# Top-k attention and an ELU feed-forward block on one core: nine transposes issued in one run, and both rows' distances formed by one GpSimd operation

## The chip, the core and the metric

The kernel runs on one core of a Trainium2 chip. The core has five engines that run their own instruction queues in order and meet through semaphores: TensorE (PE; its weight loads are shown apart as PEld), VectorE (DVE), ScalarE (ACT), GpSimd (POOL) and SyncE (SP, which issues DMAs here). The metric is the device time of one execution in microseconds; lower is better.

## The reference, cut to what matters

```python
def _attn_ref(q, k, v):                       # (8, 8, 576, 64) each
    scores = (1 / np.sqrt(64)) * np.matmul(q, k.transpose(0, 1, 3, 2))
    kth = np.partition(scores, -32, axis=-1)[..., -32:-31]
    scores = np.where(scores >= kth, scores, -1000000000.0)
    scores = scores - np.max(scores, axis=-1, keepdims=True)
    attn = np.exp(scores)
    attn = attn / (np.sum(attn, axis=-1, keepdims=True) + 1e-09)
    return np.matmul(attn, v)

def _moe_ref(x, w_in, w_out):                 # (4608, 512), (512, 2048), (2048, 512)
    h = x @ w_in
    g = np.where(h > 0.0, h, np.exp(np.minimum(h, 0.0)) - 1.0)
    return g @ w_out
```

The attention output, with its heads side by side, is `x` of the second function. All values are fp32 on the chip; the two weight matrices arrive as 64-bit floats and are decoded in the kernel.

## The kernel before

**Tiling.** For each of 8 batches the queries are cut into four tiles of 128 and one remainder of 64. A *step* is one tile and one pair of heads: `i = 0` and `i = 1` are the pair's two heads, called *row 0* and *row 1* here, each 128 x 576 scores that lie side by side in `u.sc`. A remainder's step holds four heads in two halves of the partitions. There are 144 steps. Two steps with the same pair of heads and neighbouring tiles form a *group*, whose attention product is computed at once (256 columns); remainders, and the first batch's tiles, form groups of their own.

**What a step goes through.** `scores` (L322) multiplies keys and queries into two PSUM tiles, `wide[0]` and `wide[1]`, and ACT copies them out (L339). `select` (L366) finds the 32nd largest score of each row on DVE: four rounds of MAX8 and between them three of MATCH_REPLACE8, for both rows. The first round's largest value is in `u.first`, the 32nd in `u.last`. `mask` (L389) works on one row: GpSimd forms `gap`, the 32nd score less the largest (L406); ACT then makes a steep ramp below the 32nd score (Prelu, L407) and the exponential, with its sum over the row in `u.den` (L408). `normalise` (L413) has GpSimd divide: five operations on 128 x 2 values (L418 to L423), one of them a power of 722 ns, and then one scaling of each row (L425). `turn` (L430) transposes 128 x 128 chunks of the two rows on PE (L444) and ACT copies each call's result from PSUM to the group's `et` (L445). The 1152 columns of two rows make nine chunks: `main` is chunks 0 to 3 (row 0), `rest` is chunk 4 (the last 64 columns of row 0 and the first 64 of row 1), `other` is chunks 5 to 8 (row 1). `main` and `other` take a tile of `ps_t`, a PSUM pool of two buffers that `attend` uses too; `rest` writes to spare columns of `wide[1]`. `attend` (L455) multiplies `et` with the values (L470), in pairs of row 0 and row 1, and `finish` copies the result to `xT` (L497).

**The feed-forward part.** When a block of 128 to 384 tokens has all its heads, its FFN pieces are put on a list. `hidden` multiplies with `w_in` (L545), and ACT makes the two halves of the ELU from PSUM (L555, L558) and an exponential (L560, mostly followed by a subtraction of one, L564). A *gate* closes the ELU with one addition: on GpSimd (L515) for most of the program, on DVE (L517) at the start and for the last block. `project` multiplies with `w_out` (L573), ACT copies the result (L582) and SP stores it. `feed`, called four times a step, closes the gates that are due and takes as many pieces from the list as the planner's shares allow. The pieces and their places come from fixed costs in the program, not from run time.

**What sets the order.** The first 8 steps (`tight`) have another loop, whose order is the framework's. From step 8 on, the order on PE, ACT, DVE and GpSimd is that of the source: in one round of the loop at L702 the selection of step `n` runs on DVE, the masks and the normalisation of step `n-1` on ACT and GpSimd, and the transposes of step `n-2` on PE. One round, as the queues see it:

- head: scores of step `n+2`, attention of a closed group
- feed 1, mask of row 0 of `n-1`, key and query transposes if any are due
- feed 2, `turn(done, main)`, `turn(done, rest)`, mask of row 1 of `n-1`
- feed 3, `turn(done, other)`
- normalisation of `n-1`, feed 4

Each engine takes its part of this list in order. A copy of `other` on ACT therefore stands behind the second mask's ramp and exponential and behind what feed 3 gave to ACT; a distance on GpSimd stands behind the gates that earlier feeds gave to GpSimd. For the early steps `mask` is called with `early=True`, where ACT forms the distance.

Of the kernel before, what the change touches and what calls it, by code (L numbers as in the profile page):

```python
# [9 lines left out]
ALU = mybir.AluOpType  # L10
FP32 = mybir.dt.float32
# [13 lines left out]
class Tile:  # L25
# [6 lines left out]
    def __init__(self, b, qt, rows, block, cols):  # L32
        self.b, self.qt, self.rem = b, qt, qt == 4
        self.rows = rows
        self.block = block
        self.cols = cols
        self.ql = cols.stop - cols.start
# [21 lines left out]
class Step:  # L59
# [7 lines left out]
    def __init__(self, t, hp, group, at):  # L67
        self.t, self.hp = t, hp
        self.group, self.at = group, at
        self.masked = self.normal = self.turned = False  # L70
        if t.rem:
            rows = [(4 * hp, 0), (4 * hp + 2, 0), (4 * hp + 3, 1), (4 * hp + 1, 1)]
            self.heads = [
                (h, i, slice(64 * (n % 2), 64 * (n % 2) + 64))
                for n, (h, i) in enumerate(rows)
            ]
        else:
            self.heads = [(2 * hp + i, i, slice(0, 128)) for i in range(2)]
# [3 lines left out]
def kernel(  # L82
# [9 lines left out]
    nc = tc.nc  # L92
    P = nc.NUM_PARTITIONS
    B, H, S, D = q.shape
    dm, dff = moe_w_in.shape[0], moe_w_in.shape[1] // 2
    J = S // P
# [15 lines left out]
    def pool(name, bufs, **kw):  # L112
        return ctx.enter_context(tc.tile_pool(name=name, bufs=bufs, **kw))
# [6 lines left out]
    small = pool("small", 4)  # L120
# [8 lines left out]
    early = raws.enter_context(tc.tile_pool(name="early", bufs=1))  # L129
# [69 lines left out]
    def hook():  # L199

        if not decode:
            return
        decode.pop(0)()
        if not decode:
            raws.close()
            late["f"] = ctx.enter_context(tc.tile_pool(name="f", bufs=2))
            late["g"] = ctx.enter_context(tc.tile_pool(name="g", bufs=2))
            late["x"] = ctx.enter_context(tc.tile_pool(name="xt", bufs=2))
            late["in"] = ctx.enter_context(tc.tile_pool(name="in", bufs=2))
# [103 lines left out]
    def turn_qk(whole=False):  # L313
        while turning:
            if next(turning[0], turning) is turning:
                turning.pop(0)
            elif not whole:
                return
# [3 lines left out]
    def scores(u):  # L322

        u.sc = scpool.tile([P, 2, S], FP32, tag="sc", name="sc")
        q0 = (QUERIES if u.t.b == 0 else S) + u.t.qt * P
        for half in range(2):
            for h, i, rows in u.heads:
                kq = kqT[u.t.b, h // 2]
                part = slice(i * D, (i + 1) * D)
                k0 = (KEYS if i == 0 and u.t.b == 0 else 0) + half * HS  # L330
                nc.tensor.matmul(  # L331
                    wide[i][rows, half, 0:HS],
                    kq[part, q0 : q0 + u.t.ql],
                    kq[part, k0 : k0 + HS],
                    start=True,
                    stop=True,
                )
        for i in range(2):
            nc.scalar.activation(  # L339
                u.sc[:, i, :].rearrange("p (a s) -> p a s", a=2),  # L340
                wide[i][:, :, 0:HS], AF.Copy, scale=scale,
            )
# [23 lines left out]
    def select(u):  # L366

        u.first = small.tile([P, 2, 8], FP32, tag="m1", name="m1")
        u.last = small.tile([P, 2, 8], FP32, tag="m4", name="m4")
        cur = [u.sc[:, i, :] for i in range(2)]  # L370
        found = [u.first[:, i, :] for i in range(2)]
        for i in range(2):
            nc.vector.max(found[i], cur[i])  # L373
        yield
        wk = [wkpool.tile([P, S], FP32, tag=f"wk{i}", name="wk")[:] for i in range(2)]
        for r in range(TOP_K // 8 - 1):
            for i in range(2):
                nc.vector.match_replace(wk[i], found[i], cur[i], TAKEN)  # L378
            cur = wk
            for i in range(2):  # L380
                if r < TOP_K // 8 - 2:
                    found[i] = small.tile([P, 8], FP32, tag=f"m{i}", name="m")[:]
                else:
                    found[i] = u.last[:, i, :]
                nc.vector.max(found[i], cur[i])  # L385
            hook()
            yield

    def mask(u, i, early=False):  # L389

        if u.masked:
            return
        if i == 0:
            u.den = small.tile([P, 4], FP32, tag="den", name="den")
        u.masked = i == 1  # L400
        sc, low, top = u.sc[:, i, :], u.last[:, i, 7:8], u.first[:, i, 0:1]
        gap = u.den[:, 2 + i : 3 + i]
        if early:
            nc.scalar.activation(gap, top, AF.Prelu, scale=-1.0, bias=low, alpha=1.0)
        else:
            nc.gpsimd.tensor_tensor(gap, low, top, ALU.subtract)  # L406
        nc.scalar.activation(sc, sc, AF.Prelu, scale=-1.0, bias=low, alpha=1.0 / STEEP)  # L407
        nc.scalar.activation(  # L408
            sc, sc, AF.Exp, scale=-STEEP, bias=gap, accum_out=u.den[:, i : i + 1]
        )  # L410

    def normalise(u):
# [16 lines left out]
    def turn(u, chunks):  # L429

        if u.turned:
            return
        g = u.group
        if g.et is None:
            g.et = etpool.tile([P, 2 * J + 1, len(g.tiles), P], FP32, tag="et", name="et")
        if chunks.stop - chunks.start == 1:
            ps = wide[1][:, 1, HS : HS + P]
        else:
            ps = ps_t.tile([P, JP], FP32, tag="t", name="eps")
        sc = u.sc[:, :, :].rearrange("p i s -> p (i s)")  # L440
        n = chunks.stop - chunks.start
        for c in range(n):
            c0 = (chunks.start + c) * P
            nc.tensor.transpose(ps[:, c * P : (c + 1) * P], sc[:, c0 : c0 + P], ident[:])  # L444
        nc.scalar.copy(  # L445
            g.et[:, chunks, u.at, :],
            ps[:, 0 : n * P].rearrange("p (c q) -> p c q", c=n),
        )
        if chunks.stop == 2 * J + 1:
            u.turned = True  # L450
            if u.at == len(g.tiles) - 1:
                closing.append(g)
# [149 lines left out]
    for b in range(B):  # L602
# [28 lines left out]
        for qts in order:  # L631
# [3 lines left out]
            for qt in qts:  # L635
                n = len(steps)
# [60 lines left out]
    def step(n):  # L697
        return steps[n] if 0 <= n < NS else None

    closing = []  # L700
    main, rest, other = slice(0, J), slice(J, J + 1), slice(J + 1, 2 * J + 1)
    for n in range(NS + 3):  # L702
        for fn, args in todo.pop(n, []):
            fn(*args)
        ahead, cur, prev, done = step(n + 2), step(n), step(n - 1), step(n - 2)
        if n < tight:
            turn_qk(True)
            if n < 3:
                scores(ahead)
            if n > 1:  # L710
                scores(step(n + 3))
            for i in range(2):
                passes = select_row(cur, i, n < tight - 1)
                next(passes)
                if i == 0:
                    while closing:
                        attend(closing.pop(0))
                elif prev:
                    normalise(prev)
                    turn(prev, main)  # L720
                    turn(prev, rest)
                    turn(prev, other)
                feed(n, 0.25)
                next(passes)
                mask(cur, i, True)
                feed(n, 0.25)
            continue
        if n == tight:
            ctx.enter_context(tc.manual_schedule(engines=engines))
        passes = select(cur) if cur else iter(range(4))  # L730
        if ahead and n > tight:
            scores(ahead)
        while closing:
            attend(closing.pop(0))
        next(passes)
        feed(n, 0.25)
        if prev:
            mask(prev, 0)
        turn_qk()
        next(passes)  # L740
        feed(n, 0.25)
        if done:
            turn(done, main)
            turn(done, rest)
        if prev:
            mask(prev, 1)
        next(passes)
        feed(n, 0.25)
        if done:
            turn(done, other)  # L750
        next(passes)
        if prev:
            normalise(prev)
        feed(n, 0.25)
        turn_qk(True)
# [36 lines left out]
```

## Time and profile before

| what | value |
|---|---|
| median of 3 runs | 1643.64 us (1641.84 to 1643.79) |
| the profiled execution | 1642.57 us |
| its span, first to last instruction | 1640.8 us |
| granted TensorE clock, mean | 0.974 |
| MAX8 on DVE (L385) | 816 of 752 ns |
| MATCH_REPLACE8 on DVE (L378) | 544 of 748 ns on the work copy, 272 of 748 ns on the scores |
| first FFN product on PE (L545) | 2432 of 374 ns |
| second FFN product on PE (L573) | 1152 of 599 ns |
| transposes on PE (L444) | 1152 of 279 ns into `ps_t`, 144 of 282 ns into `wide[1]` |
| copies of transposes on ACT (L445) | 288 of 571 ns, 144 of 269 ns |
| masks on ACT (L407, L408) | 288 of 782 ns, 288 of 776 ns |
| distances on GpSimd (L406) | 272 of 190 ns |
| scalings on GpSimd (L425) | 288 of 750 ns |
| gates on GpSimd (L515) | 119 of 1386 ns |

A profile shows one execution. Times in the timeline are counted from the span's start; a row there is a start, a length, the engine, the line of the source, the operation, output and inputs, how many equal instructions were merged, and in brackets how long the engine sat idle before it and what ended the idle time. The ends of matmuls are modelled, so that one that starts before its predecessor's end is the rule and not an error. PE lists 2432 first FFN products where the source has 1216, and twice the attention and second FFN products too, since each of these fp32 products is run as two instructions; a transpose is one. "A <- B" in a list of waits means that A waited and B ended it. The first 150 us are taken up by loading and decoding the weights, and there the granted clock is often half.

### The profile page before, as it was taken

What the parts mean: (1) busy time and instruction counts of PE and PEld (TensorE: products, weight loads), DVE (VectorE), ACT (ScalarE), POOL (GpSimd) and SP (SyncE); (2) the same over time, 40 slices, a digit from 0 to 9 for tenths busy, and PEclk for the clock granted to TensorE, in tenths of its full rate; (3) what the DMA queues carried; (4) which work ended last, traced back from release to release, by engine and by line L of the source; (5) the groups of instructions that cost most, each with busy time, mean ns of one, the idle gap of its engine ahead of it and who ended that gap; (6) DMA issues with size and microseconds to landing.
All of it is one profiled execution on the core that took longest, in us unless ns stands there. A gap on an engine that the chain in (4) does not pass through costs nothing.

```text
span 1640.8 us, 25344 instructions
## 1 busy us (share of the span) xinstructions
PE 1581.7 (96%) x8276; PEld 1011.8 (62%) x8276; DVE 1453.4 (89%) x2981; ACT 1187.7 (72%) x2400; POOL 708.7 (43%) x1534
## 2 busy tenths in 40 slices
PE   4788999999999999999999999999999999999999
PEld 3566777666575757555566666655557575755564
DVE  6987999999999999999999699999999599998000
ACT  6887778778695867778678686868759595958521
POOL 4775445445353534445335353535435353534300
PEclk8579999999999999999999999999999999999999
DMA  7431221012100310012100211012100201000000
GB/s 226 151 128 25 50 40 26 7 22 45 42 1 7 59 42 8 7 22 44 36 14 15 43 30 28 1 28 44 36 14 0 43 1 35 1 13 2 7 13 14
DMA packets 188037, 56.18 MB, mean 34 GB/s; under 512 B 178177, under 2 KB 179201, under 8 KB 187905
## 3 DMA queue, kind: packets, MB, share of 16 engines
q1 hardware_dynamic: 186704, 54.26, 14.1%
q8 instruction: 66, 1.08, 0.3%
q14 instruction: 67, 0.54, 0.1%
q10 hardware_dynamic: 1200, 0.30, 0.1%
HBM read 45.09 MB, written 9.44 MB: 33 GB/s over the span
## 4 chain that ended last, share of the span: by engine, by line
PE 76%; ACT 12%; DVE 7%; POOL 3%; issue 1%; DMA 1%; SPq 0%; ACTq 0%; DVEq 0%; POOLq 0%
PE ops L573 29%; PE hps L545 23%; PE avps L470 10%; PE scps L331 7%; PE eps L444 6%; DVE wk L378 3%; DVE m L385 3%; ACT sc L408 2%; ACT et L445 2%; ACT sc L407 2%; DVE m L373 1%; ACT n L564 1%; ACT n L555 1%; ACT sc L339 1%; ACT n L560 1%
## 5 line engine op out<-in xcount | busy, mean ns | idle before, releaser
L385 DVE MAX8 m<-wk 128x8 f32<-128x576 f32 x816 | 577.9, 752 | 0.3 <-POOL den L406 0.3
L545 PE MATMUL hps<-xT,w_in 128*128 128x256 f32 (+2 forms) x2432 | 545.8, 374 | 0.0
L573 PE MATMUL ops<-w_out,gT 128*128 128x512 f32 x1152 | 523.6, 599 | 0.0
L545 PEld LDWEIGHTS hps<-xT,w_in 128*128 128x128 f32 x2432 | 406.0, 192 | 100.1 <-issue 26.3
L378 DVE MATCH_REPLACE8 wk<-m,wk 128x576 f32<-128x576 f32 x544 | 401.4, 748 | 0.0
L573 PEld LDWEIGHTS ops<-w_out,gT 128*128 128x128 f32 x1152 | 209.0, 190 | 233.9 <-issue 232.8
L418 POOL TENSOR_SCALAR dene<-den 128x2 f32<-128x2 f32 x144 | 32.9, 228 | 686.5 <-ACT sc L408 686.1
L408 ACT ACTIVATE sc<-sc,den 128x576 f32<-128x576 f32 x288 | 223.6, 776 | 65.5 <-POOL den L406 44.2
L407 ACT ACTIVATE sc<-sc,m 128x576 f32<-128x576 f32 x288 | 225.3, 782 | 10.8 <-DVE m L385 10.7
L470 PE MATMUL avps<-et,vT 128*64 128x256 f32 (+2 forms) x2080 | 207.2, 330 | 17.4 <-ACT et L445 17.2
L425 POOL TENSOR_SCALAR sc<-sc,rec 128x576 f32<-128x576 f32 x288 | 213.0, 750 | 15.0 <-POOL rec L423 0.2
L331 PE MATMUL scps<-kqT 64*128 64x288 f32 (+1 forms) x1280 | 206.0, 442 | 13.6 <-ACT kqT L307 9.1
L339 ACT ACTIVATE sc<-scps 128x576 f32<-128x576 f32 x288 | 171.8, 647 | 65.1 <-PE scps L331 65.1
L445 ACT COPY et<-eps 128x512 f32<-128x512 f32 x288 | 164.6, 571 | 73.4 <-PE eps L444 73.4
L378 DVE MATCH_REPLACE8 wk<-m,sc 128x576 f32<-128x576 f32 x272 | 200.6, 748 | 0.0
L373 DVE MAX8 m<-sc 128x8 f32<-128x576 f32 x272 | 191.6, 749 | 8.8 <-ACT sc L339 8.8
L444 PEld LDWEIGHTS eps<-ident,sc 128*128 128x128 f32 x1152 | 144.9, 144 | 87.2 <-issue 52.7
L444 PE MATMUL eps<-ident,sc 128*128 128x128 f32 x1152 | 177.1, 279 | 13.7 <-POOL sc L425 13.7
L470 PEld LDWEIGHTS avps<-et,vT 128*64 128x64 f32 x2080 | 128.5, 142 | 98.8 <-ACT et L445 31.7
L515 POOL TENSOR_TENSOR gT<-n,gT 128x512 f32<-128x512 f32 (+1 forms) x119 | 164.9, 1386 | 31.2 <-ACT n L564 31.1
L331 PEld LDWEIGHTS scps<-kqT 64*128 64x128 f32 (+1 forms) x1280 | 111.3, 182 | 89.5 <-issue 43.8
L555 ACT ACTIVATE n<-hps 128x512 f32<-128x512 f32 (+1 forms) x156 | 87.3, 559 | 56.8 <-PE hps L545 56.0
(53 smaller groups left out, 1089.6 us busy)
## 6 DMA issues: line engine op xcount, KB each, us to landing
raw<-in_moe_w_in_dram SPq DMA_DIRECT2D x16, 512.0 KB, 6.1
vT<-in_v_dram SPq DMA_DIRECT2D x64, 128.0 KB, 2.5
raw<-in_moe_w_out_dram SPq DMA_DIRECT2D x16, 512.0 KB, 3.6
out_dram<-osb SPq DMA_DIRECT2D x32, 256.0 KB, 2.1
kin<-in_k_dram SPq DMA_DIRECT2D x112, 72.0 KB, 2.5
qin<-in_q_dram SPq DMA_DIRECT2D x112, 72.0 KB, 2.6
kin<-in_k_dram SPq DMA_DIRECT2D x8, 128.0 KB, 4.5
vT<-in_v_dram SPq DMA_DIRECT2D x64, 16.0 KB, 2.2
```

Of the source, the lines that this page charges most:

```text
L331: nc.tensor.matmul(wide[i][rows, half, 0:HS], kq[part, q0 : q0 + u.t.ql], kq[part, k0 : k0 + HS], start=True, stop=True,)
L373: nc.vector.max(found[i], cur[i])
L378: nc.vector.match_replace(wk[i], found[i], cur[i], TAKEN)
L385: nc.vector.max(found[i], cur[i])
L407: nc.scalar.activation(sc, sc, AF.Prelu, scale=-1.0, bias=low, alpha=1.0 / STEEP)
L408: nc.scalar.activation(sc, sc, AF.Exp, scale=-STEEP, bias=gap, accum_out=u.den[:, i : i + 1])
L425: nc.gpsimd.tensor_scalar(u.sc[:, i, :], u.sc[:, i, :], rec[:, i : i + 1], 1.0, ALU.mult, ALU.mult)
L444: nc.tensor.transpose(ps[:, c * P : (c + 1) * P], sc[:, c0 : c0 + P], ident[:])
L445: nc.scalar.copy(g.et[:, chunks, u.at, :], ps[:, 0 : n * P].rearrange("p (c q) -> p c q", c=n),)
L470: nc.tensor.matmul(ps[i * D : (i + 1) * D, cols], vt[:, 2 * J + i if c == J else i * J + c, :], w, start=(c == 0), stop=(c == J),)
L545: nc.tensor.matmul(blk.h[:, f % bank, :], w_in[:, i, f * P : (f + 1) * P], blk.xT[:, i, 0:n_tok], start=(i == 0), stop=(i == NC - 1),)
L573: nc.tensor.matmul(blk.o[:], blk.gT[f // NG][:, f % NG, s * P : (s + 1) * P], w_out[:, f, :], start=(f == 0), stop=(f == NF - 1),)
```

## The change

Two things are moved.

First, `turn(done, other)` is called right after `turn(done, main)` and ahead of `turn(done, rest)`, so that a step's nine transposes are issued in one run and their three copies stand on ACT ahead of the mask of row 1; it was called after feed 3. Since `other` is no longer the last of the three calls, `turn` counts the chunks that are left instead of asking for the last chunk's number.

Second, from step 9 on the distances of both rows are formed by one GpSimd operation on 128 x 2 values (a stride of 8 in `u.last` and `u.first`), at the head of the next round, ahead of feed 1 and its gates. It was one operation for each row, issued with that row's mask. The early steps keep the distances on ACT.

```diff
@@ Step.__init__
+        self.left = 9
@@ mask(u, i, early=False)
-        if i == 0:
+        if i == 0 and early:
             u.den = small.tile([P, 4], FP32, tag="den", name="den")
         u.masked = i == 1
         sc, low, top = u.sc[:, i, :], u.last[:, i, 7:8], u.first[:, i, 0:1]
         gap = u.den[:, 2 + i : 3 + i]
         if early:
             nc.scalar.activation(gap, top, AF.Prelu, scale=-1.0, bias=low, alpha=1.0)
-        else:
-            nc.gpsimd.tensor_tensor(gap, low, top, ALU.subtract)
...
+    def distance(u):
+
+        if u.masked:
+            return
+        u.den = small.tile([P, 4], FP32, tag="den", name="den")
+        nc.gpsimd.tensor_tensor(
+            u.den[:, 2:4], u.last[:, :, 7], u.first[:, :, 0], ALU.subtract
+        )
@@ turn(u, chunks)
-        if chunks.stop == 2 * J + 1:
+        u.left -= n
+        if u.left == 0:
             u.turned = True
@@ the loop over n, from step 8 on
+        if prev:
+            distance(prev)
         passes = select(cur) if cur else iter(range(4))
...
         if done:
             turn(done, main)
+            turn(done, other)
             turn(done, rest)
         if prev:
             mask(prev, 1)
         next(passes)
         feed(n, 0.25)
-        if done:
-            turn(done, other)
         next(passes)
```

## The prediction

> **What bounds the kernel now.** I read the page's busy shares first, then the engines' busy time by stage (start and end, length, then busy time and instruction count of PE, PEld, DVE, ACT and POOL, the granted clock, DMA).
>
> ```profile
> PE 1581.7 (96%) x8276; PEld 1011.8 (62%) x8276; DVE 1453.4 (89%) x2981; ACT 1187.7 (72%) x2400; POOL 708.7 (43%) x1534
> ...
> 200.00:450.00 250.00, 244.50 (x1575) 167.68 (x1574) 250.00 (x515) 189.97 (x385) 113.53 (x269) 0.99 0.15 31
> 450.00:600.00 150.00, 146.31 (x791) 96.01 (x790) 150.00 (x309) 115.93 (x235) 68.20 (x151) 1.00 0.11 20
> 600.00:900.00 300.00, 297.14 (x1459) 182.29 (x1460) 300.00 (x619) 223.34 (x452) 131.47 (x298) 1.00 0.11 24
> 900.00:1480.00 580.00, 578.69 (x3038) 362.82 (x3036) 544.46 (x1122) 425.98 (x862) 247.87 (x565) 1.00 0.11 23
> ```
>
> Two engines are full. DVE is busy for every microsecond of 200 to 900, so until then its pace is a floor under a step. From 900 it idles 35.5 us while PE idles 1.3: PE alone decides the end. To see where the lead changes hands I compared, step by step in the timeline, the end of a tile's selection on DVE with the start of its transposes on PE. The smallest lag is 8.0 us (tile 22: selection done 281.10, transposes 289.10); it is 12.8 at tile 44, 13.6 at tile 54 (600 us), 24 at tile 70 and 35 at tile 114. ACT's last wait of note for a selection (L407 on DVE) ended at 449.7 us. So up to about 450 us time saved on PE is mostly taken back by DVE, between 450 and 600 us up to a few microseconds, and from 600 us on it counts in full.
>
> Next, what PE waits for after the first 128 us (total us, times, longest), and two attention blocks in the timeline (start, length), one disturbed, one not:
>
> ```profile
> PE avps L470 <- ACT et L445: 13.9, 20, 2.3
> PE scps L444 <- ACT sc L339: 3.0, 6, 0.8
> PE scps L331 <- ACT et L445: 1.7, 1, 1.7
> ...
> 545.83 0.65 PE L470 MATMUL avps<-et,vT 128*64 128x256 f32 x2
> 547.01 2.37 PE L470 MATMUL avps<-et,vT 128*64 128x256 f32 x18 [0.53 <-ACT et L445]
> ...
> 816.68 2.38 PE L470 MATMUL avps<-et,vT 128*64 128x256 f32 x20
> ```
>
> The 13.9 us understate the loss: a matmul's end is modelled, and the two halves of a pair, which start 0.01 us apart when nothing holds them, are torn apart. I took the time from an attention block's first start to the start of what follows. Undisturbed it is 2.31 us (256 columns), 1.24 (128) or 1.31 (a remainder's two halves). The block at 545.83 has 549.31 - 545.83 = 3.48, so it lost 1.17, not 0.53. Over all blocks from 128 us on, leaving out the half clock in one of them, 35 are long by 0.2 us or more: 6.4 us before 200 us (4 blocks), 7.0 to 450 (7), 6.4 to 600 (6), 6.1 to 900 (7), 5.0 to 1480 (8) and 2.9 after (3); 33.9 us together. What they wait for is seen on ACT:
>
> ```profile
> 541.19 0.78 ACT L408 ACTIVATE sc<-sc,den 128x576 f32<-128x576 f32 x1
> 541.96 0.56 ACT L445 COPY et<-eps 128x512 f32<-128x512 f32 x1
> 542.43 0.26 ACT L445 COPY et<-scps 128x128 f32<-128x128 f32 x1
> 542.59 0.79 ACT L407 ACTIVATE sc<-sc,m 128x576 f32<-128x576 f32 x1
> 543.47 0.78 ACT L408 ACTIVATE sc<-sc,den 128x576 f32<-128x576 f32 x1
> ...
> 546.39 0.57 ACT L445 COPY et<-eps 128x512 f32<-128x512 f32 x1
> 546.86 1.19 ACT L339 ACTIVATE sc<-scps 128x576 f32<-128x576 f32 x2
> ```
>
> Row 1's four transposes were done at 543.04, yet their copy starts at 546.39, behind the second mask and four FFN activations. Its end, 546.96, releases the second attention matmul at 547.01.
>
> **Part 1: nine transposes together, three copies ahead of the second mask.** Nothing is added: 144 x 9 transposes at 0.109 us start to start and the same 432 copies. The built program keeps each engine's other instructions in order, and the attention matmuls after the first carry no wait of their own: what they need is covered by the score matmuls' earlier wait. Row 1's transposes and copy move past feed 3: on PE its FFN pieces, on ACT its activations, on SP nothing except one output store and one q load that change places. So the 33.9 us of attention waits go.
>
> What it adds: the remainder copy and mask 1 come one copy later, 0.47 us start to start (542.43 - 541.96). Behind them on ACT are feeds 3 and 4 and the next score copies, on GpSimd the normalisation, on PE that tile's transposes a step later. Three places could pay. (a) First transposes: from tile 53 on (91 tiles) the gap from the end of row 0's scaling to the first transpose is over 3 us in 56, 2 to 3 in 6, 1.2 to 2 in 27 and under 0.5 in 2 (tiles 69 and 105); between 450 and 600 us it is under 0.5 at two more. Only those under 0.47 pay: 2 x 0.47 = 0.9 us after 600. (b) Score matmuls wait for the remainder copy: after 600 us two blocks (685 and 749) start within 0.05 us of it, the others have 0.69 or more: 2 x 0.47 = 0.9 us. (c) PSUM for the hidden products: the smallest time from a buffer's evacuation to its next use after 150 us is 1.5 us, so 0.47 of delay plus 0.44 of transposes no longer lying between feeds 3 and 4 stays hidden: 0. If that cover were gone, up to 0.9 us in each step with 384-column FFN pieces, some 17 steps, 15 us.
>
> A cost that the trace does not price is the clock after a longer run of transposes. After 200 us the record has one drop before the last microseconds: 0.50 at 325.2 to 328.5, behind a score wait that took PE off for 1.71 us. Nine transposes last about 1.0 us. I take 0; one drop as at 325 costs half of 3.4 us, 1.7, and a drop saved gains as much.
>
> The Trainium skill (TensorE: Matmul & The Clock Gate, "Part 4: PE-mode transpose") speaks against clumping: transposes are not counted as PE activity as other matmuls are, and its "Why this matters for your kernels" warns of idle gaps over about 3 us. By the row a one-microsecond clump costs nothing. By the rule a clump adjoining a wait of over 2 us could drop the clock, and the sum would lose 1.7 us for each such place.
>
> **Part 2: one distance on GpSimd.** 272 instructions of 190 ns (L406) become 136 on 128x2. The nearest rows, L421 and L423, take 196 and 195 ns: 51.7 us become 26.7. GpSimd is 43% busy and DVE never waits for it by more than 0.3 us: 0 by itself. The order matters more:
>
> ```profile
> 540.22 0.19 POOL L406 TENSOR_TENSOR den<-m,m 128x1 f32<-128x1 f32 x1
> 540.36 1.28 POOL L515 TENSOR_TENSOR gT<-n,gT 128x512 f32<-128x512 f32 x1
> 541.59 0.20 POOL L406 TENSOR_TENSOR den<-m,m 128x1 f32<-128x1 f32 x1
> ...
> ACT sc L408 <- POOL den L406: 39.9, 43, 4.3
> ```
>
> A gate of 1.28 us can stand before a distance and hold ACT's exponential: 39.9 us in 43 waits between 450 and 1580 us. The distance now passes the gates of four feeds and, up to about 200 us, the weight decoding's operations. It is queued behind the previous tile's normalisation, as the first one was. Its new wait is for the last maximum of the step before; behind it stand the gates, and behind these the second FFN products. That maximum lies 8 us or more ahead of the first transposes, so gates should not be late. ACT idles less, but ACT at 72% does not set the end: worth 0, between -3 (waits (a) and (b) shrink) and +3 (a gate held).
>
> **The sum.** After 600 us: 6.1 + 5.0 + 2.9 = 14.0 won, 0.9 + 0.9 lost, net 12.2. Up to 600 us 19.9 us of waits go, but DVE bounds the gain: the lag can fall from 13.6 at 600 us to about 8.0 + 0.5, hence 5.1, of which I take 4.5. Before 200 us DVE waits for PE once or twice (a gate at 162.4, a key transpose at 191.7), so its unbroken run may start sooner; at 150 us the transposes wait for the scaled tile (148.78; first transpose 150.64), which leaves 1 of the 6.4 us. Together 12.2 + 4.5 + 1.0 = 17.7. The profiled execution took 1642.57 us, its span 1640.8 and 1.8 around it; the median of the runs is 1.1 higher. 1642.6 - 17.7 = 1624.9, and nearer to the median 1625.5.
>
> **The rivals.** *Full gain.* DVE's run starts earlier by most of 6.4 us and part of (a) and (b) goes with ACT's waits: 33.9 - 3 = 31, so 1612. For it: the DVE gate at 162.4 waited 5.74 us. Against it: the selection's floor up to 450 us. *Moved wait, no change.* The time won at the attention is given back at the transposes, which wait for normalisation: 1642. For it: tiles 47, 49, 69 and 105 stand there today. Against it: 62 of 91 late tiles have over 2 us. *Slower: the second mask is late.* ACT stands before row 1's copy, the mask and normalisation slide by x more than 0.47 us, and the 29 tiles with under 2 us of room (1.7 in most) wait. At 29 x (x + 0.47 - 1.7) it decides from x = 1.95, where it eats 17.7 and 3.3 more; at x = 2.2 it costs 28 and ends at 1653. For it: ACT already waited 54.4 us for transposes after 450 us. Against it: row 1's transposes take 0.44 us, less than the copy of row 0 before them. That attention still waits, now for the remainder's copy, would leave it within the likeliest case: that copy is 3 to 4 us earlier than today's last.
>
> **How the numbers follow.** Likeliest 67% (1617 to 1632), full gain 13%, no change 9%, slower 11%. A measurement of this kernel tells 0.2%, 3.3 us, from nothing. The no-change case lies near that edge and gives half of its chance to faster: faster 0.85, same 0.05, slower 0.10. The range reaches to the full gain below and almost to no change above: 1612 to 1640.
>
> **What would show it.** In the changed profile the waits of avps on et should be nearly gone, every undisturbed 256-column block 2.31 us long, the waits of the exponential on den near zero, DVE's idle time between 900 and 1480 us (35.5 us) smaller, and the first transposes' wait for the scaled tile up by a microsecond or two. I am wrong if PE's waits on scaled tiles or scores grow by over 5 us, if second FFN products begin to wait for gates, or if the clock drops more often after 200 us.

## The result, and the profile after

The changed kernel takes 1629.57 us (median of 6 runs, 1628.21 to 1631.01) against 1643.25 us before (6 runs, 1641.61 to 1644.53): a ratio of 0.9918, 95% interval 0.9905 to 0.993. It is 13.7 us faster; the forecast was 17.7 us faster. The profiled execution has a span of 1627.8 us, 13.0 less than before.

The same views as before the change, now of the changed kernel: the page's busy shares, the busy times by stage, what PE waits for from 128 to 1600 us (total us, times, longest), and ACT's wait for the distance from 450 to 1580 us. The change added lines, so L453 is now the copy of the transposes, L479 the attention, L332 the scores, L452 the transposes, L416 the distance and L407 the exponential.

```profile
PE 1573.4 (97%) x8276; PEld 1006.3 (62%) x8276; DVE 1452.7 (89%) x2981; ACT 1186.6 (73%) x2400; POOL 691.4 (42%) x1398
...
200.00:450.00 250.00, 245.53 (x1588) 169.60 (x1581) 250.00 (x515) 190.64 (x386) 109.81 (x243) 0.99 0.15 31
450.00:600.00 150.00, 147.48 (x793) 95.92 (x792) 150.00 (x311) 116.59 (x236) 67.48 (x138) 1.00 0.12 23
600.00:900.00 300.00, 298.63 (x1484) 182.96 (x1483) 300.00 (x622) 224.77 (x455) 128.33 (x270) 1.00 0.11 22
900.00:1480.00 580.00, 579.55 (x3034) 363.90 (x3032) 553.60 (x1139) 431.38 (x874) 243.40 (x513) 1.00 0.11 23
...
PE scps L332 <- ACT et L453: 6.4, 8, 2.7
PE eps L452 <- POOL sc L433: 3.8, 6, 2.1
PE scps L452 <- ACT sc L340: 0.3, 1, 0.3
...
ACT sc L407 <- POOL den L416: 58.9, 47, 4.8
```

The line that stood first, the attention's wait for the copies (13.9 us), is gone. In its place the score matmuls wait for the copies, 6.4 us where it was 1.7, and the transposes for scaled rows, 3.8 us. ACT's exponential waits longer for the distance, 58.9 us where it was 39.9. DVE is still busy without a gap to 900 us, and from 900 to 1480 us its idle time falls from 35.5 to 26.4 us, since PE holds it up less.

Lists of waits show only part of what a torn pair of matmuls costs. I therefore measured blocks from first start to next start again, and summed what is over the undisturbed length (us, blocks over by more than 0.1 us; what the half clock adds to one attention block before is left out):

| kernel, stage | attention | scores | transposes |
|---|---|---|---|
| before, 200 to 450 | 7.0 | 4.5 | 1.0 |
| after, 200 to 450 | 0 | 9.3 | 1.5 |
| before, 450 to 600 | 6.4 | 1.4 | 1.2 |
| after, 450 to 600 | 0 | 5.1 | 0.7 |
| before, from 600 | 14.0 | 1.0 | 1.6 |
| after, from 600 | 0 | 7.1 | 0.7 |

Every attention block after 150 us now has its undisturbed length. But more than half of what they won came back at the scores: from 128 us to the end the attention's losses fell from 33.9 to 4.0 us, and the scores' rose from 7.1 to 23.1. From 600 us on 16.6 us of losses became 7.8, so 8.8 us were won; the first transposes of tile 54 (at 609 us) come 4.7 us earlier than before and the end 13.0 earlier, which is 8.3 us between the two.

What the new wait is made of shows in one stretch of the changed kernel's timeline, ACT, then GpSimd, then PE (start, length, and in brackets the idle time before and what ended it):

```profile
1032.13 0.78 ACT L406 ACTIVATE sc<-sc,m 128x576 f32<-128x576 f32 x1
1033.98 0.78 ACT L407 ACTIVATE sc<-sc,den 128x576 f32<-128x576 f32 x1 [1.08 <-POOL den L416]
...
1036.91 1.06 ACT L453 COPY et<-eps 128x512 f32<-128x512 f32 x2
1037.85 0.28 ACT L453 COPY et<-scps 128x128 f32<-128x128 f32 x1
...
1031.07 1.48 POOL L433 TENSOR_SCALAR sc<-sc,rec 128x576 f32<-128x576 f32 x2
1032.52 1.28 POOL L524 TENSOR_TENSOR gT<-n,gT 128x512 f32<-128x512 f32 x1
1033.76 0.19 POOL L416 TENSOR_TENSOR den<-m,m 128x2 f32<-128x2 f32 x1
...
1037.63 1.79 PE L332 MATMUL scps<-kqT 64*128 64x288 f32 x8
1039.35 2.38 PE L479 MATMUL avps<-et,vT 128*64 128x256 f32 x20
```

The remainder's copy is last of three and ends at 1038.13. The scores, whose third matmul needs the PSUM tile that it empties, start at 1037.63 and take 1.72 us to the attention's start instead of 1.17. The copies in turn are late because the exponential ahead of them waited 1.08 us for the distance, which GpSimd formed behind the scaling of the tile before and behind a gate of 1.28 us. In the kernel before, the same exponential waited 0.58 us:

```profile
1041.82 0.78 ACT L408 ACTIVATE sc<-sc,den 128x576 f32<-128x576 f32 x1 [0.58 <-POOL den L406]
```

So a delay of the second mask goes round: normalisation later, distance later, next exponential later, copies later.

### The profile page after: what moved, and what is told of

Its sections match the earlier page's. It is cut to its first block, busy times and chain, and to the rows that moved or that the text cites. A ratio compares the mean times of both kernels' runs of the same rounds, so it can differ in the third digit from the quotient of the medians.

```text
span 1627.8 us, 25096 instructions
## 1 busy us (share of the span) xinstructions
PE 1573.4 (97%) x8276; PEld 1006.3 (62%) x8276; DVE 1452.7 (89%) x2981; ACT 1186.6 (73%) x2400; POOL 691.4 (42%) x1398
## 3 DMA queue, kind: packets, MB, share of 16 engines
q8 instruction: 66, 1.08, 0.3%
## 4 chain that ended last, share of the span: by engine, by line
PE 63%; DVE 21%; ACT 8%; POOL 4%; issue 2%; DMA 1%; SPq 0%; DVEq 0%; POOLq 0%; ACTq 0%
PE ops L582 24%; PE hps L554 20%; DVE wk L379 9%; DVE m L386 7%; PE avps L479 7%; PE scps L332 7%; PE eps L452 5%; DVE m L374 3%; ACT sc L407 2%; ACT et L453 2%; POOL sc L433 1%; ACT sc L406 1%; POOL rec L428 1%; DVE wk L355 1%; POOL w_in L194 1%
## 5 line engine op out<-in xcount | busy, mean ns | idle before, releaser
L386 DVE MAX8 m<-wk 128x8 f32<-128x576 f32 x816 | 685.7, 1017 | 0.7 <-POOL den L416 0.7
L554 PE MATMUL hps<-xT,w_in 128*128 128x256 f32 (+2 forms) x2432 | 536.4, 374 | 1.0 <-ACT gT L567 0.8
L379 DVE MATCH_REPLACE8 wk<-m,wk 128x576 f32<-128x576 f32 x544 | 472.9, 1012 | 0.0
L407 ACT ACTIVATE sc<-sc,den 128x576 f32<-128x576 f32 x288 | 224.1, 778 | 74.1 <-POOL den L416 62.9
L379 DVE MATCH_REPLACE8 wk<-m,sc 128x576 f32<-128x576 f32 x272 | 236.0, 1009 | 0.0
L332 PE MATMUL scps<-kqT 64*128 64x288 f32 (+1 forms) x1280 | 214.6, 441 | 18.7 <-ACT kqT L308 9.4
L374 DVE MAX8 m<-sc 128x8 f32<-128x576 f32 x272 | 227.3, 1011 | 5.8 <-ACT sc L340 5.8
L332 PEld LDWEIGHTS scps<-kqT 64*128 64x128 f32 (+1 forms) x1280 | 114.5, 181 | 120.3 <-issue 62.0
L479 PE MATMUL avps<-et,vT 128*64 128x256 f32 (+2 forms) x2080 | 186.1, 326 | 2.9 <-ACT et L453 2.8
L379 DVE MATCH_VALUE_LOAD wk<-m,wk 128x8 f32 x544 | 188.4, 346 | 0.0
L452 PEld LDWEIGHTS eps<-ident,sc 128*128 128x128 f32 x1152 | 137.4, 144 | 71.4 <-issue 32.5
L452 PE MATMUL eps<-ident,sc 128*128 128x128 f32 x1152 | 159.1, 280 | 19.9 <-POOL sc L433 19.4
L453 ACT COPY et<-eps 128x512 f32<-128x512 f32 x288 | 153.5, 582 | 33.7 <-PE eps L452 33.0
L479 PEld LDWEIGHTS avps<-et,vT 128*64 128x64 f32 x2080 | 118.9, 141 | 74.4 <-issue 23.7
```

The costliest lines, as they stand in the source:

```text
L332: nc.tensor.matmul(wide[i][rows, half, 0:HS], kq[part, q0 : q0 + u.t.ql], kq[part, k0 : k0 + HS], start=True, stop=True,)
L407: nc.scalar.activation(sc, sc, AF.Exp, scale=-STEEP, bias=gap, accum_out=u.den[:, i : i + 1])
L453: nc.scalar.copy(g.et[:, chunks, u.at, :], ps[:, 0 : n * P].rearrange("p (c q) -> p c q", c=n),)
L479: nc.tensor.matmul(ps[i * D : (i + 1) * D, cols], vt[:, 2 * J + i if c == J else i * J + c, :], w, start=(c == 0), stop=(c == J),)
L554: nc.tensor.matmul(blk.h[:, f % bank, :], w_in[:, i, f * P : (f + 1) * P], blk.xT[:, i, 0:n_tok], start=(i == 0), stop=(i == NC - 1),)
```

## The experiments

Each kernel was timed in five rounds beside runs of the kernel before; ratios are to these. 1642.67 us is the median before for the first four, 1642.97 us for the last four.

### One part at a time

The first part alone leaves the distances in `mask`; the second part alone leaves `turn(done, other)` behind feed 3. Against the changed kernel:

```diff
 # transposes only
-        if prev:
-            distance(prev)
...
+        else:
+            nc.gpsimd.tensor_tensor(gap, low, top, ALU.subtract)
 # distance only
             turn(done, main)
-            turn(done, other)
             turn(done, rest)
...
+        if done:
+            turn(done, other)
         next(passes)
```

> The change's first part alone: nine transposes in one run with the three copies ahead of the second mask; the two distances stay as before. Theory A (all of the gain comes from the attention's wait for row 1's copy, and GpSimd's single distance is worth nothing): within 2 us of the changed kernel, about 1629.5 us, waits of avps on et gone, and score matmuls waiting for the remainder's copy by about as much as in the changed kernel (6 us by the list of waits from 128 us on). Rival B (the single distance carries part of the gain, since it lets ACT pass its exponentials sooner): 1633 us or more.

> The change's second part alone: one distance for both rows at the head of the step; row 1's transposes and copy stay behind feed 3. Theory A: no change against the kernel before, 1643 us within 2, and the waits of avps on et stay near 14 us. Rival B: 1640 us or less. On ACT's wait for the distance: the changed kernel showed 58.9 us between 450 and 1580 us where I had forecast nearly none; if that growth comes from the normalisation being later by a copy, it stays near the 39.9 us of before here; if it comes from the single distance itself, it grows here too.

Transposes only: 1631.34 us, ratio 0.9938 (0.9926 to 0.995). Distance only: 1639.32 us, ratio 0.9981 (0.9972 to 0.9989). The product of the two ratios is 0.9919, the changed kernel's 0.9918: the parts add up. The first part brings 11.3 us, within 2 us of the changed kernel as theory A had it. The second part is worth 3.3 us, small but clear of no change; theory A had 1643 within 2 and missed, rival B's 1640 or less is met. The list of ACT's waits for a distance does not explain it: all 43 of them in the kernel before, from 450 to 1580 us, stand at row 0's exponential. What the trace shows is smaller. Row 1's exponential no longer has a semaphore to wait for, since its distance came with row 0's, and it starts 0.06 us sooner behind the ramp in every step; the attention's blocks from 600 us on lose 12.8 us instead of 14.0, 15 of the 18 long ones being shorter by 0.05 to 0.12 us. Where the other 2 us come from stays open. What PE waits for, of transposes only and then of distance only:

```profile
PE scps L332 <- ACT et L446: 8.8, 9, 2.7
PE eps L445 <- POOL sc L426: 3.9, 6, 2.1
...
PE avps L479 <- ACT et L453: 12.2, 18, 2.3
PE scps L452 <- ACT sc L340: 3.0, 6, 0.8
```

The first part alone exchanges the attention's wait for the scores' wait, a larger one than with both (8.8 against 6.4; theory A had about 6). The second part alone leaves the attention's wait (12.2). And ACT's wait for the distance, from 450 to 1580 us, is 63.1 us with the first part alone and 38.4 with the second alone, against 39.9 before and 58.9 after: it is the later mask, not the single distance, that made this wait grow.

### The order of the three copies, and the distance's place

```diff
 # remainder second
             turn(done, main)
-            turn(done, other)
             turn(done, rest)
+            turn(done, other)
 # distance sooner
-        if prev:
-            distance(prev)
         passes = select(cur) if cur else iter(range(4))
...
         if prev:
             normalise(prev)
+        if cur:
+            distance(cur)
         feed(n, 0.25)
```

> The changed kernel with the remainder chunk turned second instead of last (main, rest, other), still all ahead of the second mask. Theory A says that what the change lost against the forecast is the score matmuls' wait for the remainder's copy, which stands last of three copies: from 560 us on score blocks are long by 7.8 us in the changed kernel against 1.4 before. One copy earlier is 0.47 us earlier; blocks long by 0.56 us lose it all, those long by 0.85 to 1.6 lose 0.5: about 6 us after 450 us, so 1623.5 us. Rival C (the wait only moves to the attention or to the next transposes): within 2 us of the changed kernel, 1629.5, with avps waiting on et again.

> The changed kernel with the distance issued right behind the normalisation, ahead of feed 4, so that it no longer stands behind the gate that feed 4 gives to GpSimd (1.28 us); before 450 us this adds a wait of GpSimd for the current selection's end ahead of that gate. Theory D (a gate ahead of the distance holds ACT's first exponential, and with it the copies that the scores wait for): the waits of the exponential on den between 450 and 1580 us fall from 58.9 to under 25 us, the score blocks that are long by 0.56 us become normal, about 4 us gained, 1625.5 us. Rival E (ACT's waits there are off the path): the waits fall but the time stays within 1.5 us of 1629.5.

Remainder second: 1624.94 us, ratio 0.9892 (0.9878 to 0.9907). Distance sooner: 1623.45 us, ratio 0.9892 (0.9878 to 0.9907). Their medians lie 4.6 and 6.1 us below the changed kernel's, as theories A and D had it (by the ratios it is 4.3 us for each, and the intervals just touch the changed kernel's 0.9905 to 0.993); the rivals, a wait that only moves or lies off the path, had 1629.5. The first two lines are ACT's wait for the distance from 450 to 1580 us, of the kernel with the remainder second and of the one with the sooner distance; the last two are GpSimd's timeline in the latter.

```profile
ACT sc L407 <- POOL den L416: 60.6, 51, 4.8
...
ACT sc L407 <- POOL den L416: 20.8, 22, 3.1
...
1027.78 0.20 POOL L416 TENSOR_TENSOR den<-m,m 128x2 f32<-128x2 f32 x1
1027.93 2.51 POOL L524 TENSOR_TENSOR gT<-n,gT 128x512 f32<-128x512 f32 x2
```

With the remainder second, ACT waits as long as before (60.6) and the scores still mostly stop waiting: from 600 us on they lose 2.2 us in place of 7.1, since they need only the remainder's copy and it is one copy earlier. With the sooner distance the wait falls from 58.9 to 20.8 us, because the distance now stands ahead of the gates (1027.78 against 1027.93), and the scores lose 3.4 us from 600 us on. These are two ways to relieve the same copy.

### Both together, and the copy behind the mask

```diff
 # copy behind the mask: against the changed kernel
             turn(done, main)
-            turn(done, other)
+            turn(done, other, held)
             turn(done, rest)
         if prev:
             mask(prev, 1)
+        if done:
+            while held:
+                held.pop(0)()
```

`held` keeps row 1's copy back; its transposes stay where they were.

> The changed kernel with both of the last edits: the remainder chunk second, and the distance right behind the normalisation. Each alone took about 5 to 6 us. After 560 us the score blocks were long by 7.8 us in the changed kernel, by about 2 with the remainder second, by about 3 with the sooner distance. Theory A: both remove the same score waits, so together they add little: 1621 to 1623.5 us, with less than 1 us of PE waits after 560 us. Rival: the two are independent and add up, 1618 us or less.

> The changed kernel with row 1's copy alone put back behind the second mask on ACT (ahead of feed 3); the nine transposes stay in one run on PE, in the same place. Theory H (what pays is the copy's place on ACT, not the run of transposes on PE): the attention waits for that copy again where feed 3 gave ACT little, avps on et 4 to 9 us of waits from 128 us on, while the remainder's copy is 0.47 us sooner for the scores: about 1633 us, 1630 to 1637. Rival (the run of nine on PE is what pays): as fast as the changed kernel or faster, 1629.5 us or less, with avps on et under 2 us.

Both together: 1622.28 us, ratio 0.9874 (0.9858 to 0.989), the fastest version with the full selection, and clear of the changed kernel's interval. Theory A had 1621 to 1623.5, its rival 1618 or less. The time alone does not decide between them: by the ratios the two edits added up would give 0.9866, inside the interval measured. The traces do: from 600 us on the scores' losses fell from 7.1 us to 2.2 with the one edit, 3.4 with the other and 1.5 with both, where a sum would have left none. So the two take away mostly the same wait. What is left for PE from 560 to 1580 us:

```profile
PE eps L452 <- POOL sc L433: 0.8, 2, 0.4
PE scps L332 <- ACT et L453: 0.2, 1, 0.2
```

The copy behind the mask: 1630.29 us, ratio 0.9918 (0.9904 to 0.9933), as fast as the changed kernel, and at the near edge of what theory H gave. Its attention waits again:

```profile
PE avps L486 <- ACT et L455: 5.2, 14, 1.0
```

From 600 us on its attention loses 6.4 us where the changed kernel's loses none, and its scores 1.0 instead of 7.1. So the copy's place on ACT decides what the attention waits: ahead of feed 3 it takes the wait from 13.9 to 5.2 us, ahead of the mask it takes the rest, and this rest costs the scores about as much as it wins. Between this kernel and the one before, the transposes' place on PE and the copy's on ACT change together, so no run separates the two. The trace of the kernel before speaks against PE's order: of the 31 attention blocks that were long after 200 us, 29 stand behind a copy whose transposes had been done for 1.9 us or more, while ACT was never idle ahead of it.

### How much DVE took back

```diff
+            short = r == 1 and u.t.b > 0
-            for i in range(2):
+            for i in range(0 if short else 2):
                 nc.vector.match_replace(wk[i], found[i], cur[i], TAKEN)
             cur = wk
-            for i in range(2):
+            for i in range(0 if short else 2):
```

> The kernel before, with the second of three rounds of MATCH_REPLACE and MAX8 left out from the second batch on, so that the 24th largest score takes the place of the 32nd there and a step costs DVE four instructions less (about 2.8 us of 9.64). It is the pair of the next one: the difference of the two is what counts. Theory F (up to 450 us DVE's pace was a floor that took back what the change won on PE): the difference of the pair grows from 13 to 20 us or more. Rival G (the missing part was lost in ACT's order, not to DVE): it stays between 10 and 16 us. The time of this one alone: with the floor gone a few us below the kernel before, 1632 to 1642 us.

> The changed kernel with the same round left out, the second of three rounds of MATCH_REPLACE and MAX8 from the second batch on (24th largest score in place of the 32nd). Theory F: 20 us or more below the one before it, 1612 to 1620 us. Rival G: 10 to 16 us below it. In both DVE should show idle time between 300 and 900 us, where it has none now.

Both kernels of this pair leave out one round of the selection from the second batch on, so they give other results, and only the difference between them counts. The lighter pair: 1636.69 us for the order of before (ratio 0.9962, 0.9947 to 0.9977) and 1619.02 us for the changed order (0.9853, 0.9839 to 0.9868). The difference is 17.7 us where it is 13.7 with the full selection: neither the 20 or more of theory F nor the 10 to 16 of rival G. By the intervals the 13.7 is known to about 2 us and the 17.7 to about 3, so the times alone hardly show that they differ, and the traces have to. The busy times from 450 to 600 us, of the lighter order before and of the lighter changed one, show that the floor is gone:

```profile
450.00:600.00 150.00, 146.32 (x775) 93.09 (x774) 107.21 (x215) 112.72 (x229) 64.61 (x144) 1.00 0.13 26
...
450.00:600.00 150.00, 149.00 (x826) 95.62 (x825) 110.89 (x224) 115.45 (x235) 66.33 (x139) 1.00 0.14 27
```

DVE idles a quarter of the time in both, and PE goes from 146.3 to 149.0 of 150 us. Reading the first transposes of tiles 14 and 54 in the traces gives the size: with the lighter selection the change wins 8.9 us between the two (from +5.3 to -3.6), with the full one 3.6 (from -1.1 to -4.7). From tile 54 to the end it is 9.0 (12.6 - 3.6) and 8.3. The losses of blocks say the same: between 200 and 600 us they fall from 18.8 to 8.5 us in the lighter pair, by 10.3, and from 21.5 to 16.6 with the full selection, by 4.9. What DVE takes back passes through ACT, whose ramp waits for the selection and holds the copies behind it. From 200 to 600 us, of the kernel before, the changed one and the lighter changed one (the lighter order of before has no such wait):

```profile
ACT sc L407 <- DVE m L385: 10.7, 9, 2.2
ACT sc L406 <- DVE m L386: 25.4, 20, 4.0
ACT sc L407 <- DVE m L387: 0.2, 1, 0.2
```

So by one trace of each kernel DVE took back about 5 us, all before 600 us; the other shortfall, from 600 us on, is in both pairs.

## Why the prediction was nearly right, step by step

- **What binds.** Held. Up to 600 us DVE's pace limits what PE can win; the lighter pair measures it at about 5 us. The forecast let 4.5 us through from 200 to 600 us; between the first transposes of tiles 14 and 54 3.6 came. One reading was wrong: the smallest lag before is not tile 22's 8.0 us but tile 25's, about 7.2 (selection done 310.02, transposes 317.18). And the lag at tile 54 did not fall from 13.6 to the 8.5 of the sum, but to 10.6 (598.5, 609.1), since score blocks between 450 and 600 us lost 5.1 us.
- **The attention's waits go.** Held: 33.9 us of long blocks from 128 us on, none after 150 us now, and 14.0 of 14.0 us from 600 us on.
- **Cost (a), later transposes.** The wait held, its price did not. Tiles 69 and 105 wait for their scaled rows, 0.8 us together where 0.9 was set, and no tile after 600 us turned into a new waiter. But the transposes' losses there fell from 1.6 to 0.7 us: in the kernel before, the remainder's transpose waited for the copy of the scores at these two tiles and one other, and this wait, which the sum did not have, is gone. The first line is before, the second after, from 560 to 1580 us:

```profile
PE scps L444 <- ACT sc L339: 1.4, 3, 0.6
PE eps L452 <- POOL sc L433: 0.8, 2, 0.4
```

- **Cost (b), later score matmuls.** This is the step that failed in size. It was set at 0.9 us from 600 us on, and the scores' losses there went from 1.0 to 7.1 us: 6.1. The two blocks that the forecast named lost 0.9 more, as priced; the other 5.2 us stand in ten blocks that it had taken to have room. I had compared each block's room, 0.69 us or more in all but two, with one copy's delay of 0.47. In seven of the ten, 4.6 us together, the delay comes twice: directly, and once more through normalisation, distance and the next exponential, which stand on a loop (0.58 us of waiting became 1.08). Together it is about 0.96 against a room of about 0.8. And a third matmul held by 0.2 us tears pairs apart and costs 0.56. The kernels with the remainder second and with the sooner distance each break the loop at another place and win the time back.
- **Cost (c), hidden products, and the gates.** Held: in no list of PE's waits from 560 to 1580 us, of all these kernels, stands a hidden or a second FFN product.
- **The single distance.** Set at 0 with bounds of -3 and +3; alone it wins 3.3 us, just outside. Of this the traces show 1.2 us from 600 us on, at attention blocks, and it fits the semaphore that row 1's exponential no longer waits for; the prediction did not have this. What I said of its effect was wrong: ACT's waits for it did not fall to near zero but rose from 39.9 to 58.9 us. I had taken the gates ahead of it to be those of feeds 1 to 4, which it passes. One is not passed: feed 4's, which stands between the normalisation and the next head. Moving the distance ahead of that gate is what brought the wait down (20.8).
- **The first 200 us.** Set at 1.0; tile 14 comes 1.1 us earlier, but this agreement is luck: in the ten profiles of this study tile 8's first transposes lie between 147.1 and 153.4 us, and in the two kernels that have the same order up to there, the one before and its lighter version, at 150.6 and 147.3. That part stays open.
- **The rivals.** No change and slower are out by the time. But the moved wait of the no-change rival is there in part: time won at the attention was given back, at the scores and not at the transposes. Full gain, 1612, would have needed DVE to make room and the loop above not to close; with one of these each, the lighter changed order and the last combined version come to 1619 and 1622. Both at once were not run.
- **The signs.** The attention's waits, the block length and DVE's idle time came as forecast; the exponential's waits did not. The first sign of being wrong, waits on scaled tiles or scores up by over 5 us, is just missed by the lists (up 3.8 and 4.7 us) and clearly met by the blocks, where the scores' losses grew by 16.0 us. Up to 600 us, where they grew by 9.9, they stand where the sum had let DVE take time back; from 600 us on they are the step that failed.

The sum, for the profiled executions: from 600 us on 14.0 won at the attention and 0.9 at the transposes, less 6.1 at the scores, is 8.8 where the forecast had 12.2; the first transposes of tile 54 and the end give 8.3. From tile 14 to 54 it is 3.6 for 4.5, and before tile 14 1.1 for 1.0. Together 13.0 for 17.7. The gain of the single distance is contained in these and not added.

## What to carry to other kernels

When a copy is moved ahead of other work on an in-order engine, look for the loop that the delayed work closes: the delay may come back to the same queue a step later and count twice. Of several results that are copied out in a row, put first the one whose PSUM buffer the next matmul needs, not the one that the source names first. An operation that is issued early in the program is early only if nothing stands ahead of it in its engine's queue at that place; here one gate of 1.28 us decided.

## What the runs showed of the hardware that was not expected

**One profile can stretch one engine's lengths.** In the changed kernel's profile MAX8 has a mean of 1017 ns, in the nine others 741 to 756 ns, and small MATCH_VALUE_LOADs 342 ns against 70 to 85. In the timeline the starts keep their distance: a MAX8 pair and what follows it start 1.33 us apart in both (1001.00 to 1002.33 after, 999.69 to 1001.02 before), though each pair is shown 0.12 us longer.

```profile
1001.00 1.54 DVE L386 MAX8 m<-wk 128x8 f32<-128x576 f32 x2
1002.33 1.53 DVE L374 MAX8 m<-sc 128x8 f32<-128x576 f32 x2
...
999.69 1.42 DVE L385 MAX8 m<-wk 128x8 f32<-128x576 f32 x2
1001.02 1.41 DVE L373 MAX8 m<-sc 128x8 f32<-128x576 f32 x2
```

The first two lines are the changed kernel, the last two the kernel before. The busy time of the engine is the same to 0.7 us of 1453, so a mean length alone would have told of a slowdown of a third that did not happen.

**A distance that is long ready still costs ScalarE 0.06 us.** In the kernel before, row 1's exponential waits for a semaphore of GpSimd and starts 0.88 us after its ramp (542.59 to 543.47 in the prediction's lines), and the engine is idle for 0.09 us between the two (median of 130 steps after 200 us). With the single distance alone it has no semaphore there; it starts 0.82 us after the ramp, with 0.03 us of idle time:

```profile
542.96 0.78 ACT L406 ACTIVATE sc<-sc,m 128x576 f32<-128x576 f32 x1
543.78 0.78 ACT L407 ACTIVATE sc<-sc,den 128x576 f32<-128x576 f32 x1
```

**After 200 us the clock drops at one long wait.** In the changed kernel the scores at 271.5 us wait 2.71 us for the remainder's copy, and the granted clock is half from 276.0 us on for 3.4 us; before, it was at 325 us, behind a wait of 1.71 us. PE's timeline, then the stage behind it (the eighth value is the clock):

```profile
271.51 0.75 PE L332 MATMUL scps<-kqT 64*128 64x288 f32 x2
274.96 1.28 PE L332 MATMUL scps<-kqT 64*128 64x288 f32 x6 [2.71 <-ACT et L453]
...
276.10:279.30 3.20, 3.20 (x11) 2.54 (x11) 3.20 (x8) 2.42 (x6) 2.28 (x7) 0.50 0.00 0
```

The other runs of nine transposes, some 130 after 200 us, brought no drop until the last microseconds. Each of the eight kernels with the full selection has exactly one drop between 200 us and the last microseconds, within 1.5 us of the end of a score wait of 1.41 to 2.92 us; it lasts 3.4 us, and 6.8 in the three with the remainder second or the sooner distance. The lighter pair, with no score wait of over 1 us after 200 us, has none there at all. The length of the wait does not decide alone: in the kernel with the first part only, a wait of 1.45 us that ended at 323.2 us brought no drop. The Trainium skill (TensorE: Matmul & The Clock Gate, "Why this matters for your kernels") warns of idle gaps over about 3 us; here all of these waits are shorter by the list. That transposes do not count as activity, which the prediction had weighed from the same page's Part 4, did not show in runs of one microsecond.
